# A two-branch mixer on one core: GpSimd casts the fourth chunk of the transposed input, and the last projections ahead of the main loop run their phases in another order

## The chip, the cores and the metric

The kernel runs on one core of one Trainium2 chip. The metric is the device time of one execution in microseconds (us). Before the change the median of three runs is 735.22 us (734.99 to 735.35).

Engine names in the profile: PE is TensorE's matmuls, PEld its weight loads, DVE is VectorE, ACT is ScalarE, POOL is GpSimd, SP is SyncE, which issues all the DMAs of this kernel.

## What is computed (the reference)

The input x has 2048 tokens of 512 features. It is normalized per token; from this come two branches whose product is added to x:

```
xn = layernorm(x)
s  = attention(xn, wqkv, wo)       # 32 heads of 16, each query sees itself and the 255 keys before it
g  = silu(gelu(layernorm(xn) @ w1 + b1) @ w2 + b2)     # 512 -> 1792 -> 512
out = x + s * g
```

Everything is float32. A matmul is made of three: each operand is split into a high part (cast to the rounded type F32R) and a low part (the operand less its high part), and high by high, high by low and low by high are added up.

## The kernel before, in words

Tokens go in four chunks of 512 (c = 0 to 3), sixteen blocks of 128 (qb, kb), and heads in eight groups of four (n = 0 to 7; the four heads of n lie in one slot tile of q and k, `slots[n % 2]`). The main part is one loop over steps t from -16 to 128 (line 898). Each step issues, in this order: the probabilities of one key block for two heads (`prob_block`, p = 1; from t = 1), the maxima of a later query block (`max_block` of m = t + 12; from t = 0), the fills of half 0, the plan of step t, for t from -8 to -1 `max_block` of m, the probabilities for the other two heads (p = 0), the fills of half 1, then the product with v of the step before, and the actions put at the step's end. Every engine works through its instructions in the order in which they are issued here (class `Ordered`, line 32, holds them to program order). That helper records each instruction at line 43, so rows of the profile are told apart by tile names.

What is filled in between is written out by hand in tables: projections of q and k (`job_qk(n, c)`), of v (`job_v(hf, i)`, two key blocks each), and transposes of normalized x (`job_x(c)`). `spread` lays whole jobs over the halves of steps. `by_halves` (line 348) cuts a job of two banks into two **phases** of 24 matmuls, each on 64 of the 128 rows of TensorE: in phase 0 bank 1 is made from rows 64 to 127 and bank 0 from rows 0 to 63; in phase 1 they change rows. Phase 1 may not begin before phase 0 has gone through. What guards this is either a small instruction of another engine behind the last two matmuls of phase 0 (the "seer": a memset of one column by GpSimd or VectorE), or, without one, the last `copy_predicated` of a maxima block issued so far (`outs["max"]`).

`job_x(c)` (line 228) transposes chunk c in four groups kt of 128 features, each into one bank of PSUM. Behind a group, ScalarE casts the bank into the high part `big[:, 0, kt]` and VectorE subtracts: bank less high part gives the low part `big[:, 1, kt]`. `later(k, fn)` puts an action off by k halves of steps. The tile of all this is called xnT in the profile. The source rows of chunks 2 and 3 lie in the tile `x23`, eight blocks and one scratch block; `xs[2]` are its first four. The tile of slot 1 (tag qk1) takes the place of `x23` at step -5 (line 900), and `clear_part(k)`, k = 0 to 3, has ScalarE fill a quarter of it each (2048 columns).

`max_block(n, qb)` (line 541) makes four matmuls of scores into the tile xy and, from qb = 2, four more into zo (`first_scores`); VectorE then copies masked scores from zo into xy (COPY_PREDICATED) and reduces xy to maxima mt (TENSOR_REDUCE). There is one xy, so the next block's matmuls wait for this reduction.

The later lines of the diff are two tables of the main loop: line 822 gives the steps at which the weights of q and k of group n are split (`split_wqk`; high part by ScalarE, low part by VectorE, tile wqb), line 850 the steps at which the first-layer weights w1 of block f are split (`settle`; the high part by ScalarE at the first number). The hidden products of blocks 6 and 7 end in step 103, which copies them out by ScalarE (tile hr).

Of the kernel before, what the change touches and what calls it, by code (L numbers as in the profile page):

```python
# [9 lines left out]
F32 = mybir.dt.float32  # L10
# [40 lines left out]
def mixer_kernel(ctx, tc, x, wqk, wv, wo, w1, b1, w2, b2, out):  # L51


    nc = SimpleNamespace(**{name: Ordered(tc, name) for name in ("tensor", "vector", "scalar", "gpsimd", "sync")})
# [93 lines left out]
    def load_x(c, pools, name):  # L148
        return [load(*pools[i % len(pools)], x[512 * c + P * i: 512 * c + P * (i + 1), :], f"{name}_{c}_{i}")
                for i in range(4)]  # L150
# [4 lines left out]
    xs = {0: load_x(0, XE, "x")}  # L155
    big = bigp.tile([P, 2, KT, S], F32R, tag="big", name="xnT")
# [24 lines left out]
    fb = [psf.tile([P, 512], F32, name=f"fb{i}") for i in range(2)]  # L181
# [28 lines left out]
    mhalf = const.tile([P, 4], F32, name="mhalf")  # L210
# [13 lines left out]
    sv = small.tile([P, 32], F32, tag="sv", name="sv", bufs=1)  # L224
# [3 lines left out]
    def job_x(c):  # L228
        box = []

        def mm(k):
            kt, i = k // 4, k % 4
            if i == 0:
                box.append([fb[0], fb[1], zo[:, 0], None][kt] if c == 1 and kt < 3 or c == 3 and kt < 2 else
                           fill_bank() if c == 2 and kt in (1, 2) else
                           ps_st.tile([P, 512], F32, tag="b", name=f"tr_{c}_{kt}"))
            nc.tensor.transpose(box[kt][:, P * i: P * (i + 1)], xs[c][i][:, P * kt: P * (kt + 1)], ident)
            if i == 3:
                sl = slice(512 * c, 512 * (c + 1))
                nc.scalar.copy(big[:, 0, kt, sl], box[kt])  # L240
                later(int((c, kt) in ((2, 2), (2, 3))),
                      lambda: nc.vector.tensor_sub(big[:, 1, kt, sl], box[kt], big[:, 0, kt, sl].bitcast(F32)))
        return [(109, mm, k) for k in range(16)], lambda: None
# [37 lines left out]
    def later(k, fn):  # L281

        if k == 0:
            fn()
        else:
            h = 2 * now[0] + now[1] + k
            delayed.setdefault((h // 2, h % 2), []).append(fn)
# [60 lines left out]
    def by_halves(job, banks, first, second, seer=None):  # L348

        half, finish, box = job  # L350
        box[:] = banks
        seen = []
        for phase, where in enumerate((first, second)):
            for i in range(12):
                flags = dict(start=(phase == 0 and i == 0), stop=(phase == 1 and i == 11), skip_group_check=True)

                def unit(i=i, phase=phase, flags=flags):
                    if phase == 0 and i == 0:
                        box[:] = [bank() if callable(bank) else bank for bank in box]
                    two = (half(box[1 - phase], 1 - phase, i, slice(64, P), **flags),  # L360
                           half(box[phase], phase, i, slice(0, 64), **flags))
                    if phase == 0 and i == 11 and seer:
                        seen.append(seer[0].memset(seer[1], 0.0))
                        for r in two:
                            tc.add_manual_dep(seen[0].ins, r.ins.name, ORDER, reason="the rows are through")
                    if phase == 1 and i == 0:
                        for r in two:
                            tc.add_manual_dep(r.ins, (seen or outs["max"])[0].ins.name, ORDER, reason="the banks change rows")
                fills.setdefault(where[len(where) * i // 12], []).append((unit, ()))
        fills[second[-1]].append((finish, ()))  # L370

    def job_v(hf, i):

        box = []

        def mm(k):
            if k == 0:
                box.append(ps_st.tile([P, 2, 256], F32, tag="b", name=f"pv_{hf}_{i}"))
            j, kt, (a, b) = k // 12, k % 12 // 3, PASSES[k % 3]
            kb = 2 * i + j  # L380
            nc.tensor.matmul(box[0][:, j], big[:, a, kt, P * kb: P * (kb + 1)], wva[:, b, kt],
                             start=(k % 12 == 0), stop=(k % 12 == 11))

        def half(bank, j, k, r, **flags):
            kt, (a, b) = k // 3, PASSES[k % 3]
            kb = 2 * i + j
            return nc.tensor.matmul(bank[:, 0:256], big[r, a, kt, P * kb: P * (kb + 1)], wva[r, b, kt], **flags)

        def finish():
            if i < 4:  # L390
                nc.scalar.copy(vt[:, 2 * i: 2 * i + 2, :, 0:DH], box[0].rearrange("p b (h d) -> p b h d", d=DH))
                return
            for j, bank in enumerate(box):
                nc.scalar.copy(vt[:, 2 * i + j, :, 0:DH], bank[:, 0:256].rearrange("p (h d) -> p h d", d=DH))
        if i > 3:
            return half, finish, box
        return [(109, mm, k) for k in range(24)], finish
# [336 lines left out]
    def at(t, fn, *args):  # L734
        plan.setdefault(t, []).append((fn, args))
# [37 lines left out]
    n, raw = raws["qk"]  # L773
# [23 lines left out]
        return ps_st.tile([P, 512], F32, tag="b", name=f"pair_{now[0]}")  # L797

    others = [free_bank, free_bank]
    by_pool, by_dve = (nc.gpsimd, sv[:, 31:32]), (nc.vector, sv[:, 30:31])  # L800
    for job, banks, first, second, *seer in (
            (job_qk(0, 2), fb, [(-8, 0)], [(-7, 0)]), (job_v(0, 4), others, [(-8, 0), (-8, 1)], [(-7, 1)], by_dve),
            (job_v(0, 5), fb, [(-5, 0)], [(-4, 0)]), (job_qk(0, 3), others, [(-5, 1)], [(-4, 1)], by_pool),
            (job_v(0, 6), fb, [(-3, 0)], [(-2, 0)]), (job_qk(1, 0), others, [(-3, 1)], [(-2, 1)], by_pool),
            (job_v(0, 7), fb, [(-1, 0), (-1, 1)], [(-1, 2)], by_pool),
            (job_qk(1, 1), fb, [(0, 1), (1, 0)], [(2, 0), (2, 1)], by_pool)):
        by_halves(job, banks, first, second, *seer)
    fills.update(spread([job_x(3)], [(-6, 0), (-6, 1)]))
# [10 lines left out]
    for f, *span in ((6, 98, 103), (8, 104, 109), (10, 110, 115), (12, 116, 121, 118, 119), (2, 122, 127, 124, 125)):  # L819
        tandem(*span[:2], pair_h(f), pair_h(f + 1), *span[2:])  # L820

    for n, t in enumerate((-5, 5, 16, 28, 38, 70, 83), 1):
        at(t - 4, fetch_wqk, n)
        at(t, split_wqk, 0)
        (at if n > 1 else behind)(t + (n == 1), split_wqk, 1)
# [16 lines left out]
    on_pool = nc.gpsimd  # L842
# [5 lines left out]
                 (1, 104), (4, 104), (5, 106)):  # L848
        at(t, fetch, "w1", f)
    for f, t, lo_at, lo_by in ((6, 90, 93, nc.vector), (7, 95, 96, nc.vector), (8, 96, 98, on_pool), (9, 99, 101, nc.vector),  # L850
                               (10, 100, 102, nc.vector), (11, 103, 104, nc.vector), (12, 104, 105, on_pool),
                               (13, 105, 106, on_pool), (2, 106, 108, nc.vector), (3, 107, 109, on_pool),
                               (0, 108, 110, on_pool), (1, 110, 112, nc.vector), (4, 111, 113, on_pool),
                               (5, 112, 114, on_pool)):
        at(t, settle, "w1", f, nc.scalar.copy)
        at(lo_at, settle, "w1", f, None, lo_by)
# [41 lines left out]
    for t in range(-16, end + 1):  # L898
        m = t + LEAD
        if t == -5:  # L900
            open_slot(1)
            for k in range(4):
                at(max(-5, k - 6), clear_part, k)
        if 0 < t < end:
            prob_block(t // 16, t % 16, 1)
        if t >= 0 and m < end:
            max_block(m // 16, m % 16, m not in IN_PLACE)
        fill_in(t, 0)
        for fn, args in plan.get(t, []):
            fn(*args)  # L910
        if 4 <= m < LEAD:
            max_block(0, m)
        if 0 <= t < end:
            prob_block(t // 16, t % 16, 0)
        fill_in(t, 1)
        if t == -1:
            early.close()
            stb.append(attn.enter_context(tc.tile_pool(name="ps_s2", bufs=1, space=PSUM)).tile(
                [P, 2, 512], F32, name="stb"))
            prob_block(0, 0, 1)  # L920
            fill_in(t, 2)
        if 0 <= m < 4:
            max_block(0, m)
        if t >= 0 and m + 1 < end and (m + 1) % 16 >= 2 and m + 1 not in IN_PLACE:
            first_scores((m + 1) // 16, (m + 1) % 16)
        if t >= 1:
            pv_step((t - 1) // 16, (t - 1) % 16)
        run(lns.get(t, ()))
        if 0 <= m < end and m % 4 == 3:
            max_rows(m // 16, m % 16 // 4, t)  # L930
        for fn, args in ends.get(t, []):
            fn(*args)
# [28 lines left out]
    for f in range(6, NF, 2):  # L961
        t = gp.tile([P, 2, 512], F32, tag="ohl", name=f"hr_{f}", bufs=4)
# [199 lines left out]
    for c in range(2):  # L1162
# [30 lines left out]
        for i in range(NF + 1):  # L1193
# [29 lines left out]
            k = i - o_from  # L1223
# [141 lines left out]
    for i in range(NF):  # L1365
# [9 lines left out]
        if 5 <= i < 9:  # L1375
            raw, rec = wanted
# [37 lines left out]
```

## Time and profile before

| what | value |
|---|---|
| median of three runs | 735.22 us |
| the profiled execution's own time | 736.18 us |
| its span, first to last instruction | 734.4 us |
| PE busy | 721.2 us (98%), 7584 matmuls |
| VectorE busy | 498.6 us (68%) |
| ScalarE busy | 427.7 us (58%) |
| GpSimd busy | 319.5 us (44%) |
| chain that ended last, share on PE | 92% |
| granted TensorE clock | 1.00 throughout |

A row of the timeline reads: start, duration, engine, line, operation, written tile, read tiles, shapes and count of merged instructions, and in brackets the engine's idle time before it with what ended it. Matmuls overlap, so the distance between two starts tells how long PE took, and not the duration of a row. Step 0 begins near 61.7 us in the trace, and a step of the main loop takes some 2.8 us.

### The profile page before, as it was taken

What the parts mean: (1) busy time and instruction counts of PE and PEld (TensorE: products, weight loads), DVE (VectorE), ACT (ScalarE), POOL (GpSimd) and SP (SyncE); (2) the same over time, 40 slices, a digit from 0 to 9 for tenths busy, and PEclk for the clock granted to TensorE, in tenths of its full rate; (3) what the DMA queues carried; (4) which work ended last, traced back from release to release, by engine and by line L of the source; (5) the groups of instructions that cost most, each with busy time, mean ns of one, the idle gap of its engine ahead of it and who ended that gap; (6) DMA issues with size and microseconds to landing.
All of it is one profiled execution on the core that took longest, in us unless ns stands there. A gap on an engine that the chain in (4) does not pass through costs nothing.

```text
span 734.4 us, 19062 instructions
## 1 busy us (share of the span) xinstructions
PE 721.2 (98%) x7584; PEld 588.1 (80%) x7584; DVE 498.6 (68%) x735; ACT 427.7 (58%) x723; POOL 319.5 (44%) x675
## 2 busy tenths in 40 slices
PE   8999999999999999999999999999999999999997
PEld 8998777777778888777776788888888888888886
DVE  7877767877766676777872656546687855666833
ACT  7776777868777676788877736232343734542001
POOL 7334767867677665777877640103202000001102
PEclk9999999999999999999999999999999999999999
DMA  8324366778676733667614376447223322153701
GB/s 287 87 47 105 75 146 168 208 222 234 197 209 171 211 112 106 162 171 192 195 66 159 106 254 183 161 130 242 87 57 105 116 68 87 61 186 115 245 25 58
DMA packets 61528, 106.77 MB, mean 145 GB/s; under 512 B 12096, under 2 KB 12352, under 8 KB 61440
## 3 DMA queue, kind: packets, MB, share of 16 engines
q1 hardware_dynamic: 61440, 105.56, 48.9%
q8 instruction: 60, 0.98, 0.6%
q14 instruction: 28, 0.23, 0.1%
HBM read 54.53 MB, written 33.82 MB: 120 GB/s over the span
## 4 chain that ended last, share of the span: by engine, by line
PE 92%; ACT 3%; DVE 2%; issue 1%; DMA 1%; POOL 0%; DVEq 0%; ACTq 0%; POOLq 0%
PE fb L43 20%; PE acc L43 20%; PE zo L43 14%; PE p L43 9%; PE stb L43 9%; PE s L43 6%; PE h L43 6%; PE xy L43 5%; ACT pt L43 2%; PE pv L43 2%; DVE xy L43 1%; DVE xnT L43 1%; DVE mt L43 1%; DMA x<-in_x_dram 0%; PE tr L43 0%
## 5 line engine op out<-in xcount | busy, mean ns | idle before, releaser
L43 POOL TENSOR_SCALAR_AFFINE_SELECT pt<-pt 128x256 f32<-128x256 f32 x480 | 193.7, 429 | 99.0 <-ACT pt L43 92.3
L43 ACT ACTIVATE pt<-stb 128x768 f32<-128x768 f32 (+1 forms) x244 | 188.8, 774 | 46.1 <-PE stb L43 39.7
L43 DVE TENSOR_REDUCE mt<-xy 128x4 f32<-128x1024 f32 (+1 forms) x128 | 152.6, 1192 | 4.4
L43 DVE COPY_PREDICATED xy<-upper,zo 128x512 f32<-128x512 int32 x112 | 77.8, 695 | 74.3 <-PE xy L43 65.6
L43 POOL TENSOR_TENSOR xo<-xo,gated 128x512 f32<-128x512 f32 x15 | 20.0, 1331 | 221.7 <-DVE gated L43 220.6
L43 PE MATMUL zo<-pt,vt 128*17 128x128 f32 x2880 | 103.6, 275 | 0.1
L43 PE MATMUL stb<-qk 64*128 64x384 f32 (+1 forms) x488 | 94.8, 382 | 5.2 <-ACT pt L43 3.9
L43 PE MATMUL fb<-xnT,wqb 64*128 64x512 f32 (+2 forms) x732 | 99.7, 381 | 0.1
L43 PE MATMUL acc<-w,gh 128*128 128x512 f32 x320 | 98.4, 389 | 0.0
L43 PEld LDWEIGHTS stb<-qk 64*128 64x128 f32 x488 | 45.8, 183 | 48.5 <-ACT pt L43 39.5
L43 PEld LDWEIGHTS zo<-pt,vt 128*17 128x17 f32 x2880 | 67.5, 97 | 15.4 <-issue 4.9
L43 PEld LDWEIGHTS acc<-w,gh 128*128 128x128 f32 x320 | 60.1, 188 | 12.4
L43 PEld LDWEIGHTS fb<-xnT,wqb 64*128 64x128 f32 (+1 forms) x732 | 62.6, 185 | 6.8 <-ACT vt L43 0.4
L43 PE MATMUL acc<-w,gl 128*128 128x512 f32 x160 | 62.4, 390 | 0.2 <-DVE gl L43 0.2
L43 PE MATMUL xy<-qk 64*128 64x256 f32 (+2 forms) x536 | 58.6, 290 | 0.9 <-DVE mt L43 0.9
L43 PE MATMUL p<-xnT 128*128 128x512 f32 x189 | 51.8, 389 | 0.0
L43 PEld LDWEIGHTS xy<-qk 64*128 64x128 f32 x536 | 46.8, 185 | 6.2 <-issue 2.6
L43 ACT COPY oraw<-zo 128x128 f32<-128x128 f32 x108 | 28.8, 266 | 36.9 <-PE zo L43 28.9
L43 ACT ACTIVATE gated<-acc 128x512 f32<-128x512 f32 x16 | 8.7, 596 | 62.4 <-DVE acc L43 62.4
L43 PE MATMUL s<-wos,ohl 128*128 128x512 f32 (+1 forms) x204 | 44.3, 376 | 0.0
L43 PEld LDWEIGHTS s<-wos,ohl 128*128 128x128 f32 x204 | 36.8, 188 | 7.1
L43 PEld LDWEIGHTS p<-xnT 128*128 128x128 f32 x189 | 35.5, 188 | 7.4
(197 smaller groups left out, 1198.3 us busy)
## 6 DMA issues: line engine op xcount, KB each, us to landing
qk<-sh SPq DMA_DIRECT2D x128, 128.0 KB
qk<-pjr SPq DMA_DIRECT2D x64, 128.0 KB
oT_d<-oraw SPq DMA_DIRECT2D x32, 256.0 KB
w_d<-in_w_dram SPq DMA_DIRECT2D x14, 512.0 KB
xt_d<-xnT SPq DMA_DIRECT2D x12, 512.0 KB
x<-in_x_dram SPq DMA_DIRECT2D x16, 256.0 KB
w<-w_d SPq DMA_DIRECT2D x16, 256.0 KB
or<-oT_d SPq DMA_DIRECT2D x16, 256.0 KB
```

Source lines behind the costliest of these rows:

```text
L43: r = issue(*args, **kwargs)
```

## The change

In `job_x(3)` ScalarE copies the bank into `raw`, a block of chunk 2's normalized rows in `x23` that nobody reads any more; GpSimd casts `raw` into the high part; VectorE subtracts high part from `raw` instead of from the bank, for kt 0 and 1 half a step later than before. Since `x23` is now in use longer, the quarters of slot 1 are cleared in steps -4 (two) and -2 (two), not in -5 (two), -4 and -3.

The phases of the projections from step -5 on are laid out anew. In this table a and b are the phases 0 and 1 of a job, a1 and a2 the halves of one, and `max` is the maxima block:

| step | before | after |
|---|---|---|
| -6 | x3 (kt 0, 1), max 6, x3 (kt 2, 3) | the same |
| -5 | v5a, max 7, qk3a | v5a, max 7, v5b, qk3a |
| -4 | v5b, max 8, qk3b | v6a, max 8, qk3b, v6b1 |
| -3 | v6a, max 9, qk(1,0)a | max 9, v6b2, qk(1,0)a |
| -2 | v6b, max 10, qk(1,0)b | max 10, v7a1, qk(1,0)b |
| -1 | v7a1, max 11, v7a2, prob(0,0,1), v7b | max 11, v7a2, prob(0,0,1), v7b |

The guard of v5 becomes a small ScalarE copy (it was `outs["max"]`), that of qk(1,0) becomes `outs["max"]` (it was a GpSimd memset). In the main loop the weights of group 4 are split in step 29, not 28, and the high part of w1 block 11 is made in step 102, not 103.

```diff
@@ job_x
             if i == 3:
                 sl = slice(512 * c, 512 * (c + 1))
+                if c == 3:
+                    raw = xs[2][kt]
+                    nc.scalar.copy(raw, box[kt])
+                    nc.gpsimd.tensor_copy(big[:, 0, kt, sl], raw)
+                    later(int(kt < 2),
+                          lambda: nc.vector.tensor_sub(big[:, 1, kt, sl], raw, big[:, 0, kt, sl].bitcast(F32)))
+                    return
                 nc.scalar.copy(big[:, 0, kt, sl], box[kt])
@@ by_halves
                     if phase == 0 and i == 11 and seer:
-                        seen.append(seer[0].memset(seer[1], 0.0))
+                        seen.append(seer())
@@ the table of jobs
-    by_pool, by_dve = (nc.gpsimd, sv[:, 31:32]), (nc.vector, sv[:, 30:31])
+    by_pool, by_dve, by_act = (lambda: nc.gpsimd.memset(sv[:, 31:32], 0.0), lambda: nc.vector.memset(sv[:, 30:31], 0.0),
+                               lambda: nc.scalar.copy(sv[:, 29:30], mhalf[:, 0:1]))
...
-            (job_v(0, 5), fb, [(-5, 0)], [(-4, 0)]), (job_qk(0, 3), others, [(-5, 1)], [(-4, 1)], by_pool),
-            (job_v(0, 6), fb, [(-3, 0)], [(-2, 0)]), (job_qk(1, 0), others, [(-3, 1)], [(-2, 1)], by_pool),
-            (job_v(0, 7), fb, [(-1, 0), (-1, 1)], [(-1, 2)], by_pool),
+            (job_v(0, 5), fb, [(-5, 0)], [(-5, 1)], by_act), (job_qk(0, 3), others, [(-5, 1)], [(-4, 1)], by_pool),
+            (job_v(0, 6), fb, [(-4, 0)], [(-4, 1), (-3, 1)]), (job_v(0, 7), fb, [(-2, 1), (-1, 1)], [(-1, 2)], by_pool),
+            (job_qk(1, 0), others, [(-3, 1)], [(-2, 1)]),
@@ main loop tables
-    for n, t in enumerate((-5, 5, 16, 28, 38, 70, 83), 1):
+    for n, t in enumerate((-5, 5, 16, 29, 38, 70, 83), 1):
...
-                               (10, 100, 102, nc.vector), (11, 103, 104, nc.vector), (12, 104, 105, on_pool),
+                               (10, 100, 102, nc.vector), (11, 102, 104, nc.vector), (12, 104, 105, on_pool),
@@ step -5
-                at(max(-5, k - 6), clear_part, k)
+                at(-4 + k // 2 * 2, clear_part, k)
```

## The prediction, made before the changed kernel had run

> **What bounds the kernel now.** I read three things in order: the page's busy shares, the list of what TensorE waited for, and the timeline of steps -6 to 0, engine by engine.
>
> ```profile
> PE 721.2 (98%) x7584; PEld 588.1 (80%) x7584; DVE 498.6 (68%) x735; ACT 427.7 (58%) x723; POOL 319.5 (44%) x675
> ```
>
> ```profile
> PE stb L43 <- ACT pt L43: 3.9, 13, 0.4
> PE xy L43 <- DVE mt L43: 0.9, 3, 0.4
> ```
>
> TensorE is the bound nearly throughout, and the change leaves it the same matmuls. It can only win stalls back or make new ones. The two largest of the main stretch (total, times, longest) are small, and all idle time of TensorE is 734.4 - 721.2 = 13.2. So the sum is one of tenths of a microsecond, in the one stretch that the change rebuilds.
>
> ```profile
> 45.05 1.68 PE L43 MATMUL fb<-wva,xnT 64*128 64x256 f32 x24
> 46.91 0.50 PE L43 MATMUL xy<-qk 64*128 64x256 f32 x4 [0.18 <-DVE mt L43]
> ...
> 48.10 0.38 PE L43 MATMUL pair_-5_786<-xnT,wqb 64*128 64x256 f32 x1 [0.21 <-DVE xnT L43]
> ...
> 49.52 1.71 PE L43 MATMUL fb<-wva,xnT 64*128 64x256 f32 x24
> 50.96 0.51 PE L43 MATMUL xy<-qk 64*128 64x256 f32 x4
> ...
> 52.86 1.71 PE L43 MATMUL fb<-wva,xnT 64*128 64x256 f32 x24
> ```
>
> ```profile
> 60.38 0.51 PE L43 MATMUL xy<-qk 64*128 64x256 f32 x4
> ...
> 60.89 0.93 PE L43 MATMUL fb<-wva,xnT 64*128 64x256 f32 x12
> 61.66 0.34 PE L43 MATMUL stb<-qk 64*128 64x384 f32 x2
> 62.10 1.69 PE L43 MATMUL fb<-wva,xnT 64*128 64x256 f32 x24
> ```
>
> Starts tell the price here, not durations. A phase takes 1.44 (49.52 to 50.96); a maxima block with the phase behind it takes 1.90 (50.96 to 52.86), so the block alone 0.46. From v5a at 45.05 to the first probabilities (stb) at 61.66 there are nine phases and five blocks: 9 x 1.44 + 5 x 0.46 = 15.26, and it took 16.61. So 1.35 is lost at most. Two places hold most of it: max 7 starts at 46.91 where 45.05 + 1.44 = 46.49 would do (0.42), and from there to v5b at 49.52 max 7 and qk3a take 2.61 for 1.90 (0.71).
>
> ```profile
> 44.91 0.69 DVE L43 COPY_PREDICATED xy<-upper,zo 128x512 f32<-128x512 int32 x1
> 45.63 1.23 DVE L43 TENSOR_REDUCE mt<-xy 128x4 f32<-128x1024 f32 x1
> 46.77 1.28 DVE L43 TENSOR_TENSOR xnT<-tr,xnT 128x512 fp32r<-128x512 f32 x2
> ```
>
> ```profile
> 51.69 0.70 DVE L43 COPY_PREDICATED xy<-upper,zo 128x512 f32<-128x512 int32 x1 [1.11 <-PE zo L43]
> 52.42 1.23 DVE L43 TENSOR_REDUCE mt<-xy 128x4 f32<-128x1024 f32 x1
> ```
>
> VectorE causes both. Max 6 was reduced until 45.63 + 1.23 = 46.86, and 0.05 later max 7 starts. The subtractions of the third and fourth transposed bank end at 46.77 + 1.28 = 48.05, and 0.05 later the second bank of qk3 is free.
>
> **The change, part by part.**
>
> *Max 6 no longer stands behind subtractions.* They now come after it on VectorE, half a step later.
>
> ```profile
> 43.75 0.34 PE L43 MATMUL zo<-qk 64*128 64x128 f32 x4
> ```
>
> ```profile
> 43.08 1.07 ACT L43 CAST xnT<-fb 128x512 fp32r<-128x512 f32 x2
> 44.71 1.08 ACT L43 CAST xnT<-tr 128x512 fp32r<-128x512 f32 x2 [0.56 <-PE tr L43]
> ...
> 46.19 3.72 ACT L43 ACTIVATE qk<-vt 128x2048 fp32r<-128x2048 f32 x2
> ```
>
> Max 6's matmuls end at 43.75 + 0.34 = 44.09; the reduction then ends at 44.13 + 0.72 + 1.23 = 46.09, and max 7 can start at 46.49 with v5a's end. That stall of 0.42 goes. ScalarE's copies cost what its casts do, so the banks are free at 44.15 and 45.79, long before qk3a: the 0.71 goes too.
>
> *Four copies on GpSimd are new.* The trace has no such copy of 512 columns.
>
> ```profile
> 49.85 0.10 POOL L43 MEMSET sv<- 128x1 f32 x1 [6.59 <-PE pair_-5_786 L43]
> ```
>
> ```profile
> 61.95 0.10 POOL L43 MEMSET sv<- 128x1 f32 x1 [5.26 <-PE fb L43]
> ```
>
> ```profile
> L43 POOL TENSOR_SCALAR x<-x,nm,rss 128x512 f32<-128x512 f32 x5 | 3.8, 771 | 0.0
> L43 POOL MEMSET qk<- 128x1024 f32 x1 | 1.0, 953 | 0.0
> ```
>
> ```profile
> 144.87 1.28 POOL L43 TENSOR_TENSOR pjr<-pjr,sh 128x512 fp32r<-128x512 f32 x1
> ```
>
> Below stands half of the memset of 1024 columns, 0.48; above the two-input subtraction, 1.28. I take 0.77, the row with one streamed input, as the copy has. GpSimd is idle from 43.26 to 49.85, so nothing waits behind the copies there. From the first bank copied (43.67) they end at 44.5, 45.3, 46.1 and 46.9. VectorE's four subtractions follow the reduction of max 6 from 46.09, behind them max 7's masked copy and reduction.
>
> ```profile
> L43 DVE TENSOR_TENSOR wqb<-wqkr,wqb x7: 679/681/1281, 53.6 to 300.7; 128x512 fp32r<-128x512 f32 x7
> ```
>
> ```profile
> 145.44 1.26 DVE L43 TENSOR_TENSOR wqb<-wqkr,wqb 128x512 fp32r<-128x512 f32 x1
> ```
>
> They now have both inputs in SBUF, as wqb's have (shortest, median and longest in ns in the row above): 0.68 alone, 1.26 at 145.44, in the middle of GpSimd's subtraction, which ends at 146.15, 0.6 before wqb's does. With one such meeting, at the fourth copy, four take 0.68 x 4 + 0.58 = 3.3 and end at 49.3. Max 7 is then reduced by 51.3, and max 8 wants to start at 51.42. qk3a, from 48.54, wants the last low part at 48.54 + 11 x 0.12 = 49.9. Both fit, by 0.1 and 0.6.
>
> The Trainium skill, page "SBUF — State Buffer", section "SBUF: two separate sides", has a rule that speaks against the change: a VectorE instruction with two SBUF inputs and a GpSimd instruction that reads SBUF exclude one another for their whole length. The two wqb rows agree with it. By it the subtractions could each meet a copy; what that gives here is the slower rival below.
>
> *The guard of v5 goes over ScalarE.* TensorE waits for it with everything behind. The trace shows the like for GpSimd: v7's a2 ends at 60.89 + 0.93 = 61.82, memset 61.95 to 62.05, phase b at 62.10.
>
> ```profile
> L43 ACT ACTIVATION_READ_ACCUMULATOR x<-x 128x1 f32 x7 | 1.4, 200 | 0.0
> ```
>
> For a ScalarE copy of one column I put 0.20 for the 0.10: 0.38 from end to start. Between nothing and a copy of 0.27 the stall is 0 to 0.25. v5a ends at 46.73, so v5b starts at 47.11, where 46.49 + 0.46 = 46.95 would do: minus 0.16. ScalarE has only the wqb cast and v5's copies behind the guard, wanted after 48.8.
>
> *Maxima a phase and a half apart.* By the rows at 50.96, 51.69 and 52.42 a block's matmuls and its reduction take 0.73 + 1.96 + 0.05 = 2.74 before the next block may start. One and a half phases and a block take 2.16 + 0.46 = 2.62. So from max 8 on VectorE is late by 0.12 each time. Replayed: max 8 at 51.42, qk3b 51.88, v6b1 53.32, max 9 wanted at 54.04 and let in at 54.16; v6b2 54.62, qk(1,0)a 55.34, max 10 wanted at 56.78, let in at 56.90; v7a1 57.36. Then qk(1,0)b is wanted at 58.08, but its guard is now max 10's masked copy: 56.90 + 0.73 + 0.70 + 0.05 = 58.38, so 0.30 more. Max 11 follows at 59.82 without a wait, and the first probabilities 1.28 later as before (60.38 to 61.66): **61.10 instead of 61.66, a gain of 0.56**.
>
> *Cleared quarters move.* ScalarE does two from 49.45 (after v5's copies) to 53.2 and two from 56.2 to 59.95; its next copies are wanted at 53.6 and 60.1. I cost them at nothing: TensorE's phases hide them, with 0.1 to spare at the second pair; uncovered, the first exponential comes late by what runs over. The sends by SP of qk(1,0) start some 0.3 later, and nobody reads that slot before step 4.
>
> *Step 103 loses a cast.*
>
> ```profile
> 355.59 0.85 PE L43 MATMUL zo<-pt,vt 128*17 128x128 f32 x24
> 356.84 0.44 PE L43 MATMUL stb<-qk 64*128 64x384 f32 x2 [0.40 <-ACT pt L43]
> ```
>
> ```profile
> 352.37 0.81 ACT L43 ACTIVATE pt<-stb 128x768 f32<-128x768 f32 x1 [0.54 <-PE stb L43]
> ...
> 355.45 0.62 ACT L43 CAST xnT<-xnT 128x512 fp32r<-128x512 f32 x1
> ```
>
> The cast at 355.45 is block 11's. Without it the exponential behind it starts some 0.5 earlier and TensorE's wait of 0.40 goes. In step 102 the cast falls into the 0.54 that ScalarE idles ahead of 352.37; it takes about that, so at most 0.1 comes back. **Gain 0.40.** Moving group 4's weights from step 28 to 29 saves VectorE the meeting at 145.44; no wait of TensorE stands there, so I take 0, between a loss and a gain of 0.1.
>
> **Sum:** 0.56 + 0.40 = 0.96, against the profiled execution's 736.18 (734.4 and 1.8 around it), which lies 0.96 above the median of 735.22. Taken from the median: **734.2 us**.
>
> **The rivals.**
>
> *VectorE keeps up (0.17).* If the wait for reductions (0.12 twice) and the two guards (0.16 and 0.30) cost nothing, the stretch gains 0.56 + 0.70 = 1.26, with step 103 1.7: 733.5. For it speaks that waits of 0.12 are no more than rows of one kind differ by (max 11 with half a phase took 1.28 for 1.18); against it that four waits have to vanish.
>
> *Slower: the copies and subtractions exclude one another (0.13).* Place: VectorE between the reductions of max 6 and max 7. At 1.28 a copy, with GpSimd and VectorE taking turns, the copies end at 45.0, 46.3, 48.2 and 50.1 and the subtractions at 51.3. qk3a waits for the fourth high part (wanted at 48.54 + 6 x 0.12 = 49.3, 0.85 late) and its low part (about 0.5), max 8 for a reduction that ends at 53.3 (0.4 or so). That is 1.8 more stall; 0.56 - 1.8 + 0.40 = -0.9: 736.1. It decides from about 1.1 us a copy on, where the stall passes 0.96. For it: two-input rows at 1.28 and the wqb row at 1.26. Against: one streamed input, and GpSimd's row for that says 0.77.
>
> *The change doesn't do what it says (0.15).* If subtractions that end late let max 8 wait by some 0.5, the stall has only moved from max 7 to max 8, and step 103 alone counts: 734.8.
>
> **How the numbers follow.** Forecast 0.50, rivals 0.17, 0.13 and 0.15, anything worse 0.05. The range goes from 733.3 (the first rival less the 0.2 of small terms) to 736.1 (the bound of the copies). Within 0.2% (1.47 us), about what a measurement can tell from no change: the forecast, the last two rivals, and a little of the first: 0.78. Faster by more: most of the first and a tail of the forecast, 0.17. Slower by more: 0.05.
>
> **What would show it.** In the new trace: no wait for mt ahead of max 7, none for xnT ahead of qk3a; GpSimd copies near 0.77, one stretched; waits of 0.1 for mt ahead of max 9 and 10 and one of 0.3 for xy ahead of qk(1,0)b; first probabilities near 61.1; no wait near 356. Copies over 1.1 us, a late max 8, or ScalarE's clearing under way when the first exponential is due would make it wrong.

## The result, and the profile after

| | before | changed |
|---|---|---|
| median of 14 runs each, us | 735.03 (734.74 to 735.61) | 733.74 (733.37 to 734.12) |
| ratio to before, 95% interval | | 0.9981 (0.9973 to 0.9989) |
| span of the profiled execution, us | 734.4 | 732.0 |

The changed kernel is 1.29 us faster, which is just under the 0.2% of the forecast; the forecast was 0.96.

The two spans differ by 2.4, more than the medians. TensorE's row of v5a shows why: it starts at 45.05 before and at 44.20 after, and max 5's masked copy, ahead of everything that the diff touches, already starts at 41.02 and 40.18. These 0.85 belong to the two executions, not to the change: among the kernels below, e10, which is built on the changed one, starts v5a at 45.03, and all others between 43.8 and 44.3, e3 and e4 among them, which change nothing ahead of the main loop. What sets this start was not looked into. So stretches are compared from v5a on.

TensorE's timeline of the changed kernel, steps -5 to -1 (start, duration, engine, operation, tile):

```profile
44.20 1.70 PE L43 MATMUL fb<-wva,xnT 64*128 64x256 f32 x24
45.73 0.40 PE L43 MATMUL xy<-qk 64*128 64x256 f32 x4
...
46.18 1.69 PE L43 MATMUL fb<-wva,xnT 64*128 64x256 f32 x24
...
50.59 0.40 PE L43 MATMUL xy<-qk 64*128 64x256 f32 x4
50.83 0.34 PE L43 MATMUL zo<-qk 64*128 64x128 f32 x4
...
53.23 0.51 PE L43 MATMUL xy<-qk 64*128 64x256 f32 x4
53.57 0.34 PE L43 MATMUL zo<-qk 64*128 64x128 f32 x4
...
55.96 0.51 PE L43 MATMUL xy<-qk 64*128 64x256 f32 x4
...
56.48 0.93 PE L43 MATMUL fb<-wva,xnT 64*128 64x256 f32 x12
57.44 0.38 PE L43 MATMUL pair_-3_956<-xnT,wqb 64*128 64x256 f32 x1
...
58.97 0.40 PE L43 MATMUL xy<-qk 64*128 64x256 f32 x4
...
60.15 0.34 PE L43 MATMUL stb<-qk 64*128 64x384 f32 x2
```

From v5a to the first probabilities it takes 60.15 - 44.20 = 15.95, where it took 61.66 - 45.05 = 16.61: **0.66 won**. The bracketed waits ahead of max 7 (46.91 before) and of qk3a (48.10 before) are gone.

VectorE and GpSimd of the same stretch:

```profile
43.28 0.70 DVE L43 COPY_PREDICATED xy<-upper,zo 128x512 f32<-128x512 int32 x1 [1.15 <-PE zo L43]
44.01 1.23 DVE L43 TENSOR_REDUCE mt<-xy 128x4 f32<-128x1024 f32 x1
45.16 2.88 DVE L43 TENSOR_TENSOR xnT<-x,xnT 128x512 fp32r<-128x512 f32 x4
47.95 0.68 DVE L43 COPY_PREDICATED xy<-upper,zo 128x512 f32<-128x512 int32 x1
48.67 1.23 DVE L43 TENSOR_REDUCE mt<-xy 128x4 f32<-128x1024 f32 x1
```

```profile
42.89 1.17 POOL L43 CAST xnT<-x 128x512 fp32r<-128x512 f32 x2 [0.47 <-ACT x L43]
44.51 1.17 POOL L43 CAST xnT<-x 128x512 fp32r<-128x512 f32 x2 [0.45 <-ACT x L43]
```

Max 6's masked copy now comes ahead of all four subtractions. They end at 48.04, and max 7's reduction at 49.90, 0.7 before max 8 starts at 50.59.

The two places in the main loop (steps 28 and 29 together, and step 103), by the rows of the probabilities with which a step begins (p = 1), first before, then after:

```profile
142.77 0.44 PE L43 MATMUL stb<-qk 64*128 64x384 f32 x2
...
148.61 0.39 PE L43 MATMUL stb<-qk 64*128 64x256 f32 x2
...
353.57 0.44 PE L43 MATMUL stb<-qk 64*128 64x384 f32 x2
```

```profile
141.25 0.44 PE L43 MATMUL stb<-qk 64*128 64x384 f32 x2
...
146.93 0.39 PE L43 MATMUL stb<-qk 64*128 64x256 f32 x2
...
351.81 0.44 PE L43 MATMUL stb<-qk 64*128 64x384 f32 x2
...
354.62 0.44 PE L43 MATMUL stb<-qk 64*128 64x384 f32 x2
```

Step 103 took 356.84 - 353.57 = 3.27 and takes 354.62 - 351.81 = 2.81: **0.46 won**. Steps 28 and 29 took 5.84 and take 5.68: **0.16 won**. Together 0.66 + 0.46 + 0.16 = 1.28, against 1.29 by the medians. That the two meet to a hundredth is luck: from v5a to the last instruction the two executions differ by 1.5, so some 0.2 of their difference lies at none of these places.

### The profile page after: what moved, and what is told of

Same layout as the page of the kernel before. It is cut to its first block, busy times and chain, and to the rows that moved or that the text cites. A ratio compares the mean times of both kernels' runs of the same rounds, so it can differ in the third digit from the quotient of the medians.

```text
span 732.0 us, 19063 instructions
## 1 busy us (share of the span) xinstructions
PE 719.5 (98%) x7584; PEld 586.1 (80%) x7584; DVE 496.5 (68%) x735; ACT 427.7 (58%) x724; POOL 321.6 (44%) x678
## 4 chain that ended last, share of the span: by engine, by line
PE 92%; ACT 3%; DVE 2%; DMA 1%; issue 1%; POOL 0%; SPq 0%; DVEq 0%; ACTq 0%; POOLq 0%
PE acc L43 20%; PE fb L43 20%; PE zo L43 13%; PE stb L43 9%; PE p L43 9%; PE s L43 6%; PE h L43 6%; PE xy L43 5%; ACT pt L43 3%; PE pv L43 2%; DMA qk<-pjr 1%; DVE xy L43 0%; DMA x<-in_x_dram 0%; DVE bn L43 0%; DVE mt L43 0%
## 5 line engine op out<-in xcount | busy, mean ns | idle before, releaser
L43 PE MATMUL s<-wos,ohl 128*128 128x512 f32 (+1 forms) x204 | 44.3, 376 | 0.0
```

The lines of the kernel that those rows point to most:

```text
L43: r = issue(*args, **kwargs)
```

## The experiments

The theory was that the price lies in waits on VectorE, and that each part of the change takes its own away. Rivals were that the cast brings all, that the order brings all, or that only the main-loop tables do. All kernels were timed against the kernel before; its medians in these sessions lay between 735.07 and 735.20.

| kernel | median, us | ratio, 95% interval | v5a to first probabilities |
|---|---|---|---|
| before | 735.03 | 1 | 16.61 |
| changed | 733.74 | 0.9981 (0.9973 to 0.9989) | 15.95 |
| e1, cast alone | 737.55 | 1.0034 (1.0021 to 1.0048) | 18.98 |
| e2, order alone | 734.99 | 0.9998 (0.9989 to 1.0007) | 16.29 |
| e3, step 102 alone | 734.46 | 0.9991 (0.9982 to 0.9999) | |
| e4, step 29 alone | 734.92 | 0.9997 (0.9988 to 1.0006) | |
| e5, guard back | 733.53 | 0.9978 (0.9969 to 0.9987) | 15.78 |
| e6, each cast twice | 735.28 | 1.0001 (0.9993 to 1.0010) | 17.13 |
| e7, two phases apart | 734.46 | 0.9991 (0.9982 to 1.0000) | 16.53 |
| e8, cast alone, GpSimd clears | 736.53 | 1.0013 (1.0004 to 1.0022) | 18.04 |
| e10, even spacing | 733.35 | 0.9975 (0.9965 to 0.9984) | 15.43 |

Each ratio is to before in its own session. Intervals of some 0.1% to either side are 0.7 us, so terms of 0.1 to 0.4 are read from the timelines, and the times only have to agree.

**e1: the cast alone.** Before, with the new `if c == 3` block of `job_x` and `at(-4 + k // 2 * 2, clear_part, k)`; the tables stay.

> The kernel before with the GpSimd cast and the moved clearing alone; phases and main-loop tables as before. Theory (waits on VectorE are the price, and each part takes its own): max 7 starts with v5a's end (0.3 to 0.4 less), but qk3a comes half a step earlier than in the changed kernel and waits for its last low part by some 0.5, about as before; gain 0.45, about 734.6 us. Rival (the cast brings everything, the order of phases nothing): the stretch from v5a to the first probabilities takes 15.95 as in the changed kernel, gain 0.66, 734.4.

It was 2.5 us slower; both expectations fell. TensorE and ScalarE of this kernel, which starts v5a at 44.22 and max 8 at 50.25:

```profile
48.11 0.38 PE L43 MATMUL pair_-5_789<-xnT,wqb 64*128 64x256 f32 x1 [0.22 <-DVE xnT L43]
...
55.02 0.38 PE L43 MATMUL pair_-3_930<-xnT,wqb 64*128 64x256 f32 x1 [0.85 <-ACT pjr L43]
...
63.20 0.44 PE L43 MATMUL stb<-qk 64*128 64x384 f32 x2 [0.86 <-ACT pjr L43]
```

```profile
50.98 3.72 ACT L43 ACTIVATE qk<-vt 128x2048 fp32r<-128x2048 f32 x2
...
58.89 3.72 ACT L43 ACTIVATE qk<-vt 128x2048 fp32r<-128x2048 f32 x2
62.50 0.37 ACT L43 COPY pjr<-pair_-3_929 128x256 f32<-128x256 f32 x1
```

The first row is the wait for the low part that the theory had. The two waits of 0.85 are new: a pair of clearings (50.98) stands ahead of the copies that empty qk3's banks, and another (58.89) ahead of those of qk(1,0), and the next user of the bank waits. From max 8 on the stretch is 2.25 longer than before (12.95 for 10.70), practically all of it at these two places if starts are compared. Ahead of max 8, where no clearing is under way yet, it is 0.12 longer (6.03 from v5a for 5.91): max 7 starts 0.33 earlier, but qk3a, right behind it, comes too early for the subtractions and gives that back. In the changed kernel the pairs stand in front of the same copies, but they follow v5's and v6's copies, and these come earlier in the new order, so each pair is over when the next copy is due.

**e8: the cast alone, clearing by GpSimd.** As e1, with one more line:

```diff
-        nc.scalar.activation(flat, vt[:, 0, 0, DH: DH + 1].to_broadcast([P, 2048]), AF.Identity, scale=float(k >= 2))
+        nc.gpsimd.memset(flat.bitcast(F32), float(k >= 2))
```

> The cast alone (phases and main-loop tables as before) with the four quarters of slot 1 cleared by GpSimd memsets instead of ScalarE, at the same steps. Theory (the cast alone was 2.5 slower because the clearing, which has to come later, holds ScalarE's copies out of the banks): the two waits of 0.85 for pjr go, the stretch from v5a to the first probabilities falls from 18.98 to some 16.6 or less, 734.6 to 735.1 us. Rival (the cast itself is too late for the old order of phases): about 737 as with the cast alone.

The waits for pjr went, as the theory said, but only 0.94 of the stretch came back, not 2.4. A new wait stands ahead of max 9 (TensorE, GpSimd, VectorE of this kernel):

```profile
54.14 0.50 PE L43 MATMUL xy<-qk 64*128 64x256 f32 x4 [0.78 <-DVE mt L43]
```

```profile
48.19 3.55 POOL L43 MEMSET qk<- 128x2048 f32 x2
```

```profile
49.55 2.22 DVE L43 CAST mh<-mt 128x16 fp32r<-128x16 f32 x1
```

VectorE's cast of 16 columns, 0.17 to 0.28 in the kernel before, ends at 51.77, when GpSimd's second memset ends (48.19 + 3.55 = 51.74), and max 8's reduction is behind it. So e8 swaps one obstacle for another. It shows that the clearing on ScalarE made the two waits. The rival has a part too: up to max 8 e8 takes 6.04, like e1, where before took 5.91, so in the old order the cast wins nothing there, whichever engine clears. What it would bring with the clearing out of everybody's way was not tried; by these stretches (18.98 less 2.25) I estimate 16.7, no better than before.

**e2: the order alone.** The changed kernel without the `if c == 3` block and with 28 and 103 in the tables.

> The changed kernel without the cast on GpSimd and without the two entries of the main-loop tables: the new order of phases alone. Theory: max 7 waits for max 6's reduction as before (0.3 to 0.4), qk3a waits no more; stretch 16.35, gain 0.26, about 734.8 us. Rival (the order brings everything): stretch 15.95, 734.4. Rival (spacing of one and a half phases costs what the order saves): stretch 16.6, 735.0.

The stretch takes 60.28 - 43.99 = 16.29, a gain of 0.32, nearest to the theory's 0.26; max 7 still waits for max 6's reduction (0.17 of idle time in the row), qk3a waits no more. The time cannot tell 0.3 from nothing.

**e3 and e4: the two entries of the main loop**, each alone: `(11, 102, 104` for `(11, 103, 104`, and 29 for 28.

> The kernel before with block 11's high part in step 102 alone. Theory: the wait of 0.40 for the exponential near 356 goes and the step behind it shortens by 0.46; 734.57 us. Rival (the wait comes back in step 102 or is made up for later): 735.0.

> The kernel before with group 4's weights split in step 29 alone. Theory as predicted: nothing, 735.03 us within 0.1. Rival (steps 28 and 29 together took 5.84 before and 5.68 in the changed kernel, so the meeting with GpSimd cost 0.16): 734.87.

In e3 step 103 takes 355.64 - 352.84 = 2.80, 0.47 less, step 102 takes 3.05 for 3.04, and the time falls by 0.61: the wait does not come back. In e4 steps 28 and 29 take 147.29 - 141.62 = 5.67, 0.17 less. The time (0.15 less) is too coarse for this, but the same two steps took 5.68 in the changed kernel, so the rival holds and not the nothing that I forecast.

**e6: each cast twice.**

```diff
                     nc.gpsimd.tensor_copy(big[:, 0, kt, sl], raw)
+                    nc.gpsimd.tensor_copy(big[:, 0, kt, sl], raw)
```

> The changed kernel with every one of the four GpSimd casts made twice, 1.18 us a bank instead of 0.59. Theory with exclusion (a subtraction with two SBUF inputs and a GpSimd read shut one another out): GpSimd ends near 49.7 on the clock where v5a starts at 44.2, subtractions near 50.4, qk3a and max 8 wait, 1.2 to 1.7 slower than the changed kernel, 735.0 to 735.4 us. Rival without exclusion: GpSimd ends at 47.6, subtractions at 48.3, all within what max 8 leaves: 733.74.

The stretch took 1.18 more than in the changed kernel, just under what exclusion gives, and the ratio moved from 0.9981 to 1.0001; the time of 735.28 lies inside what exclusion gives. GpSimd, VectorE and TensorE of e6, the second and third fence one instruction to a row:

```profile
42.84 6.13 POOL L43 CAST xnT<-x 128x512 fp32r<-128x512 f32 x8 [0.46 <-ACT x L43]
```

```profile
45.30 1.07 POOL L43 CAST xnT<-x 128x512 fp32r<-128x512 f32 x1
46.44 0.95 POOL L43 CAST xnT<-x 128x512 fp32r<-128x512 f32 x1
...
48.02 0.95 POOL L43 CAST xnT<-x 128x512 fp32r<-128x512 f32 x1
```

```profile
45.10 0.80 DVE L43 TENSOR_TENSOR xnT<-x,xnT 128x512 fp32r<-128x512 f32 x1
45.82 1.09 DVE L43 TENSOR_TENSOR xnT<-x,xnT 128x512 fp32r<-128x512 f32 x1
47.43 1.07 DVE L43 TENSOR_TENSOR xnT<-x,xnT 128x512 fp32r<-128x512 f32 x1 [0.51 <-POOL xnT L43]
49.00 0.69 DVE L43 TENSOR_TENSOR xnT<-x,xnT 128x512 fp32r<-128x512 f32 x1 [0.51 <-POOL xnT L43]
```

```profile
49.02 0.38 PE L43 MATMUL pair_-5_820<-xnT,wqb 64*128 64x256 f32 x1 [0.48 <-POOL xnT L43]
```

Five of the eight casts take their usual 0.61, the three shown 0.95 to 1.07; three subtractions take 0.80 to 1.09, and only the last, which no cast meets, takes 0.69. They take turns: the subtraction of 45.10 ends at 45.90, the cast behind it at 46.37, the next subtraction at 46.91, the next cast at 47.39, each about half a microsecond behind the one that it met. The casts end at 48.97, between the 47.6 without exclusion and the 49.7 that I gave with it. qk3a waits for the last high part and max 8 for a late reduction, which are the places that the slower rival named. Twice the price of the copies gives back all that the change won.

**e5 and e7: guard and spacing.** e5 puts `by_pool` back behind qk(1,0)'s entry. e7 does this too and moves v6:

```diff
-(job_v(0, 6), fb, [(-4, 0)], [(-4, 1), (-3, 1)])
+(job_v(0, 6), fb, [(-4, 1)], [(-3, 1)], by_pool)
```

> The changed kernel with the GpSimd memset put back as the guard of qk(1,0). Theory (its phase 1 waits 0.3 for max 10's masked copy): the step from v7a1 to max 11 shortens by 0.3, maxima 10 and 11 come as close as 2.74, about 733.45 us. Rival (max 11 then waits for max 10's reduction by what is saved): 733.74 as the changed kernel.

> The changed kernel with qk(1,0)'s guard on GpSimd and v6's phases a step half later (v6a behind qk3b, v6b behind max 9, guard on GpSimd), so that maxima 7 to 10 are two phases apart. Theory (one and a half phases leave VectorE late by 0.1 each time, the guard by 0.3): 0.2 less than with the guard alone, 0.5 less than the changed kernel, 733.25 us. Rival (the spacing costs nothing): as with the guard alone, 733.45.

In e5 the stretch is 0.17 shorter, half of what I expected: qk(1,0)b does not wait, but max 11 starts at 58.77, 2.74 behind max 10, and its first four matmuls take 0.34 up to the next row and not 0.24, like those of maxima 9 and 10. Theory and rival each have half. e7 is 0.9 slower than e5, against my expectation; VectorE and TensorE of e7:

```profile
48.59 1.23 DVE L43 TENSOR_REDUCE mt<-xy 128x4 f32<-128x1024 f32 x1
```

```profile
49.88 0.51 PE L43 MATMUL xy<-qk 64*128 64x256 f32 x4 [0.64 <-DVE mt L43]
```

Max 7's reduction stands behind the four subtractions and ends at 49.82. With two phases between max 7 and max 8 TensorE arrives too early. The three phases that the change leaves there are not slack: they are the subtractions' cover, and the phase and a half elsewhere pays for them.

**e10: even spacing.** From e5, v6a leaves a quarter for the half behind max 8, in front of qk3b; v6b comes in thirds and v7a in two parts. A first version, e9, left v6 without a guard of its own, so that nothing held its phase 1 behind its phase 0; it has no time. e10 adds the guard:

```diff
-(job_v(0, 6), fb, [(-4, 0)], [(-4, 1), (-3, 1)]), (job_v(0, 7), fb, [(-2, 1), (-1, 1)], [(-1, 2)], by_pool),
+(job_v(0, 6), fb, [(-4, 0)] * 3 + [(-4, 1)], [(-4, 1)] + [(-3, 1)] * 2, by_pool),
+(job_v(0, 7), fb, [(-2, 1)] * 2 + [(-1, 1)], [(-1, 2)], by_pool),
...
+    fills[-4, 1][:0] = fills[-4, 1][13:16]
+    del fills[-4, 1][16:19]
```

> The changed kernel with the guards of qk(1,0) and v6 on GpSimd and the units of v6 and v7 spread so that maxima 7 to 8 are 2.75 phases apart, 8 to 9 1.58, 9 to 10 1.67 and 10 to 11 1.67. Theory (VectorE needs 2.74 us from one maxima block to the next, and more between 7 and 8, where it subtracts): no block comes late, the stretch from v5a to the first probabilities takes 15.45 instead of 15.78 with qk(1,0)'s guard alone and 15.95 in the changed kernel; 733.2 us. Rival (the spacing is not what makes those blocks take 0.51 instead of 0.42): 15.78, 733.5.

```profile
45.03 1.70 PE L43 MATMUL fb<-wva,xnT 64*128 64x256 f32 x24
...
53.81 0.40 PE L43 MATMUL xy<-qk 64*128 64x256 f32 x4
54.05 0.33 PE L43 MATMUL zo<-qk 64*128 64x128 f32 x4
...
60.46 0.40 PE L43 MATMUL stb<-qk 64*128 64x384 f32 x2
```

The stretch takes 15.43, and each of these blocks takes 0.24 up to its next row (53.81 to 54.05). At 733.35 us, 0.9975 of before (0.9965 to 0.9984), it is the fastest median of the study; that it beats before is clear, that it beats the changed kernel by 0.4 lies inside the intervals and is borne out by the timeline alone.

## Why the prediction was right, point by point

- **Max 6 ahead of the subtractions, qk3a behind v5b:** as forecast. Both waits went.
- **The copies:** a cast takes 0.61, and two in a row 1.17, between my bounds of 0.48 and 1.28 and below the 0.77 that I took. The one meeting came at the fourth copy, as the sum had it: that copy runs until 45.68 (44.51 + 1.17), and the first subtraction, begun at 45.16, takes 1.07 for 0.68. The four take 2.88 together for my 3.3, since the meeting cost 0.4 and not 0.58 and the others start 0.6 apart, so max 8 had 0.7 to spare and not 0.1. The rule of the Trainium skill's page "SBUF — State Buffer", section "SBUF: two separate sides", that I set against the change is borne out by this meeting and by e6, where the two engines take turns; here it cost TensorE nothing, because max 8 came late enough.
- **The guard of v5 on ScalarE, put at 0.16:** max 7 and v5b start 0.45 apart, so nothing was lost at the guard itself; its phase then took 1.53 (46.18 to 47.71) for 1.44. v5a took 1.53 too (44.20 to 45.73), which the sum did not have, and the two together make up the 0.16 and a little more. That max 8 starts 6.39 behind v5a, for 6.37 in the replay, is partly luck.
- **One and a half phases, put at 0.12 late for max 9 and 10:** they show no idle time, but their first four matmuls took 0.34 up to the next row where max 8's took 0.24; e10 has both back. The size was right, the form was not a wait.
- **qk(1,0)'s guard, put at 0.30:** the weight load of its phase 1 waits 0.23 for max 10's masked copy and the phase takes 1.53 (57.44 to 58.97), which comes to that, but without them (e5) only 0.17 is won, because max 11 is late instead.
- **The end of the stretch:** the replay has max 11 14.77 behind v5a, and that is where it starts; the first probabilities follow 1.18 later and not 1.28. The 1.28 was copied from before, where max 11 came due just as max 10's reduction ended (59.10 + 1.23 = 60.33, start 60.38) and paid that 0.1; I had seen the 1.28 for 1.18 and taken it for scatter. This is the whole of the 0.10 that the stretch won beyond the forecast.
- **The clearing, put at nothing:** right here, with 0.2 to spare ahead of the copy at 59.17. I gave its price as "what runs over"; e1 shows that it is 0.85 twice in another order of phases. The cast (with the clearing that it pushes back) and the order are not two parts to be added: alone they bring -2.5 and next to nothing by the clock.
- **Step 103, 0.40:** 0.46. **Group 4's weights, put at 0 within 0.1:** mis-sized; 0.16 or 0.17. I read no wait at 147.46, but VectorE's masked copy had ended at 147.41, and the row started when it did, with 0.37 from it to the next row, where the changed kernel takes 0.27: a delay can stand in start times and not in a bracket.

The sum was 0.96 and came out as 1.28, by 0.10 behind max 11, 0.06 in step 103 and 0.16 at group 4's weights, which all went one way. By the time alone the rival in which VectorE keeps up (733.5) is nearer to 733.74 than my 734.2; the timeline speaks for the forecast, since the stretch won 0.66, not that rival's 1.26, and the terms that had to vanish in it were paid. Max 8 did not wait, as the last rival had it. The slower rival needed copies of 1.1; with two casts of 0.61 to a bank it happens (e6). Two of my sums are a tenth off by rounding: 735.22 - 0.96 is 734.26, and the slower rival's 0.56 - 1.8 + 0.40 is -0.84.

ScalarE's rows behind the point on the clearing, the subtraction that met the fourth copy, and the load that waited for qk(1,0)'s guard, all of the changed kernel:

```profile
55.24 3.72 ACT L43 ACTIVATE qk<-vt 128x2048 fp32r<-128x2048 f32 x2
59.17 0.37 ACT L43 COPY pjr<-pair_-3_956 128x256 f32<-128x256 f32 x1 [0.21 <-PE pair_-3_957 L43]
```

```profile
45.16 1.07 DVE L43 TENSOR_TENSOR xnT<-x,xnT 128x512 fp32r<-128x512 f32 x1
```

```profile
57.43 0.18 PEld L43 LDWEIGHTS pair_-3_956<-xnT,wqb 64*128 64x128 f32 x1 [0.23 <-DVE xy L43]
```

Rows of the kernel before, behind the points on the end of the stretch (max 10's reduction) and on group 4's weights:

```profile
59.10 1.23 DVE L43 TENSOR_REDUCE mt<-xy 128x4 f32<-128x1024 f32 x1
```

```profile
146.75 0.66 DVE L43 COPY_PREDICATED xy<-upper,zo 128x512 f32<-128x512 int32 x1
```

```profile
147.46 0.44 PE L43 MATMUL zo<-qk 64*128 64x128 f32 x4
```

## What to carry to other kernels

When one step of a chain is moved to an idle engine, look at what keeps its buffers longer and what must wait for them: here the cast alone lost 2.5 us, nearly all of it to a clearing that it pushed back, and paid only together with an order of work that makes room for it. An uneven spacing may be the cover of something; replay the engine that sets it through the whole interval before evening it out. A price of nothing needs its cover named, and a wait that shows no idle time can still be seen by comparing the distance of the same two rows.

## What the runs showed of the hardware

In this kernel a block that comes due just as its release arrives pays about 0.1 without idling. In the changed kernel TensorE's weight loads of max 8 start 0.11 ahead of its matmuls, those of max 9 at the same time, 0.05 behind the end of max 8's reduction (51.95 + 1.23 = 53.18):

```profile
50.48 0.31 PEld L43 LDWEIGHTS xy<-qk 64*128 64x128 f32 x4
...
53.23 0.30 PEld L43 LDWEIGHTS xy<-qk 64*128 64x128 f32 x4
```

The wait holds the weight load back, so the loads lose their head start, and the first matmuls come further apart: 0.34 to the next row (53.23 to 53.57) for 0.24 (50.59 to 50.83). The durations in the rows do not show this reliably: before, max 8 (50.96) has 0.51 as well, but its next row follows at 51.20, 0.24 later. The 1.53 of v5a and v5b goes with the same sign, loads that start with their matmuls (44.19 and 44.20, both 46.18).

In e8 two GpSimd memsets back to back held a tiny VectorE cast, begun in the first, until the second ended: 2.22 for 0.17. The reduction ahead of that cast (48.29, 1.23 long) ran beside the first memset at its usual length. That the memsets are the cause rests on the two ends falling together, in this one place.
